# Attention into a snake feed-forward block on one core: opening loads and copies dealt out anew, batch 1's loads and steps reordered

## The chip, the core and the metric

The kernel runs on one core of a Trainium2 chip. The metric is the device time of one execution in microseconds (us), lower is better. Three runs of the kernel before gave 283.33, 283.48 and 284.21 us; their median, 283.48 us, is the time before.

The engines go by the names of the profile: PE is TensorE's matrix multiply and PEld its weight load, DVE is VectorE, ACT is ScalarE, POOL is GpSimd, SP is SyncE, which here only issues transfers. Each engine works through its own list of instructions in the order in which the program names them, and waits at an instruction until its inputs are there and its output buffer is free.

## The reference

Linear attention over 8 batches of 8 heads, 576 positions and 64 columns, and then a feed-forward block with the activation h + sin²(alpha·h)/alpha on the 4608 tokens that come out:

```python
q_s = exp(q - max(q, axis=-1));  q_s = q_s / (sum(q_s, axis=-1) + 1e-09)
k_s = exp(k - max(k, axis=2));   k_s = k_s / (sum(k_s, axis=2) + 1e-09)
kv  = einsum('bhsd,bhse->bhde', k_s, v)
x   = einsum('bhsd,bhde->bhse', q_s, kv)        # (8, 8, 576, 64), taken as 4608 x 512
h   = x @ w_in                                  # w_in 512 x 2048
s   = sin(alpha * h)
g   = h + s * s / (alpha + 1e-09)
out = g @ w_out                                 # w_out 2048 x 512
```

All inputs and the output are float32 in memory; the kernel multiplies in bfloat16.

## The kernel before

**Tiling.** A batch's 576 positions are laid out as 64 groups of 9 (`j`), two heads side by side on the 128 partitions. The feed-forward block runs over 9 token tiles `t` of 512 tokens. For each tile there are 16 blocks `ni` of 128 columns of w_in: `mm_h` (line 254) makes one block of h with four matmuls over the four row blocks `k` of w_in, in the order `KO` = 0, 2, 1, 3. `sine` (line 265) takes the sine on ACT and squares it on ACT, POOL or DVE, and `combine` (line 276) makes g on DVE, which also frees the accumulator bank of h. Then 64 matmuls `mm_o` (line 280), called output products here, multiply g with w_out into four accumulators, and `evac_o` copies and stores them.

**Attention of one batch.** `exp_half` takes exponentials of q or k on ACT, for one half `ii` of the heads. `norm_q` normalises q on DVE and POOL into `qn`. `cast_v0` and `cast_v1` turn v into bfloat16 (`vb`). `kv_mm` (36 small matmuls for a half) multiplies k and v, `kv_norm` divides on DVE and gives `kbd`. `q_transpose_ii` turns `qn` on TensorE, a copy makes `qT` of it. `attn_x` multiplies `qT` and `kbd`, and copies put the result into `xT`, the input of `mm_h`.

**The opening** (lines 305 to 410). SP loads q, k and v of batch 0 in halves. POOL waits for the first half of k (`held`, line 338, a copy of one column whose only use is that the loads behind it on POOL are not issued before) and then issues the second half of v in two parts, and w_in through `load_win`, which converts to bfloat16 on the way: columns 0 to 255 of row blocks 0 and 2, the same columns of row blocks 1 and 3, then 256 columns at a time up to 1023. After its cast of v it issues w_in's columns 1024 to 1535 and 1536 to 2047 and w_out's row blocks 0 to 3 and 4 to 7. TensorE multiplies the blocks `ni` 0 to 3 with row blocks 0 and 2 first ("early products", lines 401 to 410), since `xT` for these is made first, from half 0 of the heads. The main loop adds row blocks 1 and 3 (line 413).

**Tile 0's blocks** (lines 457 to 463). The loop over `ni` issues the blocks; the table `late` (line 457) names loads that are issued behind a block: behind `ni` 6 the first half of batch 1's q on SP, behind 8 and 10 w_out's row blocks 8 to 11 and 12, 13 on POOL, behind 13 the second half of q and all of k and v of batch 1. `load_q1` (line 441) first writes one column on DVE, so that SP's issue waits for DVE's place in the program.

**Batch 1** (lines 465 to 514). `o_quad` hands out tile 0's 64 output products, and `take(os, n)` puts the next n of them on TensorE. The order of the products is written out: products 1 to 16 use w_out's row blocks 0 to 3, 17 to 32 use 4 to 7, 33 to 48 use 8 to 11, 49 to 56 use 12 and 13, the rest 14 and 15. After the first 46 come batch 1's transposes, `kv_mm`, `attn_x` (in `x_half`), with the other 18 between them. Then `mm_h(1, 0)`, the first block of tile 1, follows. Within this stretch POOL makes the first half of `qn`, waits for k's first half (`held`, line 471) and issues w_out's row blocks 14 and 15.

Of the kernel before, what the change touches and what calls it, by code (L numbers as in the profile page):

```python
# [23 lines left out]
def kernel(  # L24
# [23 lines left out]
    MF = 512  # L48
# [57 lines left out]
    def load_win(c0, c1, cc=slice(0, 4)):  # L106
        nc.gpsimd.dma_start(out=win[:, cc, c0:c1], in_=win_v[:, cc, c0:c1])

    def load_wout(n0, n1):
        nc.gpsimd.dma_start(out=wout[:, n0:n1, :], in_=wout_v[:, n0:n1, :])  # L110
# [13 lines left out]
    def exp_half(name, b, ii, j1=J, j0=0):  # L124
        if (name + "e", b) not in A:
            A[name + "e", b] = att2.tile([128, J, 4 * D], BF16, name=name + "e")
        exp_to(A[name + "e", b][:, j0:j1], staged[name, b][:, :, j0:j1], (ii,))
# [10 lines left out]
    def norm_q(b, engs, j1=J):  # L138

        qe = A["qe", b][:, 0:j1].rearrange("p j (ii x d) -> p ii j x d", ii=2, x=2)  # L140
        A["qn", b] = qn = att1.tile([128, 2, J, 2 * D], BF16, name="qn")
        qs = small.tile([128, J, 4], F32, name="qs")
        if len(engs) == 1:
            nc.vector.tensor_reduce(qs, A["qe", b].rearrange("p j (i d) -> p j i d", i=4), axis=AXL.X, op=ALU.add)  # L144
            nc.vector.reciprocal(qs, qs)  # L145
        for ii in range(2):
            part = qs[:, 0:j1, 2 * ii:2 * ii + 2]
            if len(engs) == 2:
                nc.vector.tensor_reduce(part, qe[:, ii], axis=AXL.X, op=ALU.add)  # L149
                nc.vector.reciprocal(part, part)  # L150
            engs[ii % len(engs)].tensor_tensor(qn[:, ii, 0:j1].rearrange("p j (x d) -> p j x d", x=2), qe[:, ii],  # L151
                                               part.unsqueeze(3).to_broadcast([128, j1, 2, D]), op=ALU.mult)
# [101 lines left out]
    def mm_h(t, ni, k0=0, k1=4):  # L254

        if ni == 0 and k0 == 0:
            G[t] = gpool.tile([128, nN, MF], BF16, name="g")
        hp = HP[t, ni] if k0 else bank(BANKS.get(t, 3 * "aabb" + "abba")[ni])
        HP[t, ni] = hp
        for k in range(k0, k1):  # L260
            nc.tensor.matmul(hp, win[:, KO[k], ni * 128:(ni + 1) * 128],  # L261
                             xT[:, KO[k], t * MF % NX:t * MF % NX + MF], start=(k == 0), stop=(k == 3))
        return hp
# [69 lines left out]
    def cast_v0(ii, j0, j1, eng):  # L333
        vv = vb[0].rearrange("p j (i c) -> p i j c", i=4)
        eng(vv[:, 2 * ii:2 * ii + 2, j0:j1, 0:D], staged["v", 0][:, ii::2, j0:j1])  # L335
# [2 lines left out]
    GP_CP(held, staged["k", 0][:, 0, 0, 0:1])  # L338
    load0(GP, "v", v, 1, 0, 5)
    load0(GP, "v", v, 1, 5, 9)  # L340
    for ii in range(2):
        load_win(0, 256, slice(ii, 4, 2))
    for c in range(1, 4):
        load_win(256 * c, 256 * c + 256)

    def warm_up(n):
# [36 lines left out]
    kv_norm(0, 0, 1)  # L383
    tp1 = ps_l.tile([128, 8, 128], BF16, name="tp", tag="l")
    q_transpose_ii(0, 1, 0, 8, tp1)
    cast_v0(1, 0, 5, DVE_CP)
    cast_v0(1, 5, 9, GP_CP)
    for c in range(2, 4):
        load_win(512 * c, 512 * c + 512)
# [2 lines left out]

    xp = [bank("b") for _ in range(2)]
    attn_x(0, 0, 0, 8, xp)
    DVE_CP(xT[:, 0, 0:MF], xp[0])
    ACT_CP(xT[:, 2, 0:MF], xp[1])
    ACT_CP(A["qT", 0][:, 1, 0:8], tp1)
    nc.scalar.activation(zero, zero, AX.Sin)
    kv_mm(0, 1, ps_k, split=True)
    kv_norm(0, 1, 2)  # L400
    for ki in range(2):
        for ni in range(2):
            mm_h(0, ni, ki, ki + 1)
    xp = [bank("l") for _ in range(2)]
    attn_x(0, 1, 0, 8, xp)
    for x in range(2):
        DVE_CP(xT[:, 2 * x + 1, 0:MF], xp[x])
    for ki in range(2):
        for ni in range(2, 4):
            mm_h(0, ni, ki, ki + 1)  # L410

    def h_slot(t, ni, sq, lag):
        hp = mm_h(t, ni, 2 if ni < (4, 1, 0)[min(t, 2)] else 0)
# [18 lines left out]
    def take(it, n=1000):  # L432
        for _ in range(n):
            if next(it, 0) == 0:
                return
# [4 lines left out]
    with ES:  # L440
        def load_q1(ii):
            if ii == 0:
                staged["q", 1] = stage.tile([128, 4, J, D], F32, name="st_q", tag="st")
            st = staged["q", 1]
            DVE_CP(st[:, ii, 0, 0:1], zero)
            nc.sync.dma_start(out=st[:, ii::2, 0:8].rearrange("p i j d -> p i (j d)"),
                              in_=src_view(q, 1)[:, ii::2, 0:8 * D])

        def load_kv1():
            for n in "kv":  # L450
                staged[n, 1] = stage.tile([128, 4, J, D], F32, name=f"st_{n}", tag="st")
            for ii in range(2):
                for n, t in (("k", k), ("v", v)):
                    nc.sync.dma_start(out=staged[n, 1][:, ii::2].rearrange("p i j d -> p i (j d)"),
                                      in_=src_view(t, 1)[:, ii::2])

        late = {6: lambda: load_q1(0), 8: lambda: load_wout(8, 12), 10: lambda: load_wout(12, 14), 13: lambda: (load_q1(1), load_kv1())}
        for ni in range(nN):
            h_slot(0, ni, "DPPAPPAPPAAPPAPD"[ni], lag)
            flush(lag, 1)  # L460
            if ni in late:
                late[ni]()
        flush(lag, 0)

        accs = [bank(kind) for kind in "bbll"]
        os = o_quad(0, accs, [DVE_CP, ACT_CP, DVE_CP, DVE_CP])
        take(os, 46)
        for ii in range(2):
            exp_half("q", 1, ii, 8)
        norm_q(1, [GP, V], 8)  # L470
        GP_CP(held, staged["k", 1][:, 0, 0, 0:1])
        load_wout(14, 16)

        def cast_v1(ii, eng):
            vv = vb[1].rearrange("p j (i c) -> p i j c", i=4)
            eng(vv[:, 2 * ii:2 * ii + 2, :, 0:D], staged["v", 1][:, ii::2])

        exp_half("k", 1, 0)
        cast_v1(0, ACT_CP)
        exp_half("k", 1, 1)  # L480
        def transpose_q1(ii):
            tp = ps_h[0].tile([128, 8, 128], BF16, name="tp", tag="a")
            q_transpose_ii(1, ii, 0, 8, tp)
            DVE_CP(q_tile(1)[:, ii, 0:8], tp)

        transpose_q1(0)
        take(os, 4)

        def x_half(ii):
            xp = [bank("a") for _ in range(2)]  # L490
            attn_x(1, ii, 0, 8, xp)
            for x in range(2):
                (ACT_CP, DVE_CP)[x](xT[:, 2 * x + ii, MF:2 * MF], xp[x])

        kv_mm(1, 0, ps_k, split=True)
        kv_norm(1, 0, 1)
        for b in range(2):
            DVE_CP(q8[:, 0, b, 0:1], zero)
            nc.sync.dma_start(out=q8[:, :, b], in_=src_view(q, b)[:, :, 8 * D:J * D])
        load_batch(2)  # L500
        cast_v1(1, DVE_CP)
        take(os, 4)
        x_half(0)
        take(os, 2)
        transpose_q1(1)
        kv_mm(1, 1, ps_k, split=True)
        kv_norm(1, 1, 2)
        take(os, 5)
        x_half(1)
        exp_to(A["qe", 1][:, J - 2:J], q8)  # L510
        nc.scalar.activation(zero, zero, AX.Sin)
        take(os)
        for ki in range(2):
            mm_h(1, 0, ki, ki + 1)
        norm_q8()
        load("q", q, 3)
        load("k", k, 3)
        load("v", v, 3)

        def late_q8(ni):  # L520
            if ni == 11:
                tp = ps_k.tile([128, 2, 2, 128], BF16, name="tp", tag="a")
                for b in range(2):
                    for ii in range(2):
                        nc.tensor.transpose(tp[:, ii, b], A["qe", 1][:, J - 2 + b, ii * 128:(ii + 1) * 128], identb)
                DVE_CP(A["qT", 1][:, :, J - 2:J], tp)
            elif ni == 15:
                xp = ps_k.tile([128, 2, 512], F32, name="xp", tag="a")
                for ii in range(2):
                    for b in range(2):  # L530
                        for e in range(2):
                            for x in range(2):
                                r, c = slice(64 * x, 64 * x + 64), (2 * ii + b) * P
                                nc.tensor.matmul(xp[64 * e:64 * e + 64, x, c:c + P], kbd[b][r, e, ii],
                                                 A["qT", 1][r, ii, J - 2 + b, e * 64:(e + 1) * 64],
                                                 start=True, stop=True)
                DVE_CP(xT[:, :, 16 * P:18 * P].rearrange("p (x i) n -> p x i n", x=2),
                       xp[:, :, 0:4 * P].rearrange("p x (i n) -> p x i n", i=2))

        for ni in range(nN):  # L540
            h_slot(1, ni, SQ[ni], lag)
            flush(lag, 1)
            late_q8(ni)
        cast_v(2, [GP_CP, GP_CP])
        flush(lag, 0)
# [149 lines left out]
```

## Time and profile before

| what | value |
|---|---|
| runs | 283.33, 283.48, 284.21 us |
| profiled execution | 284.08 us |
| its span on the core | 282.3 us |
| HBM read, written | 36.71 MB, 9.44 MB |
| w_in's pieces, issue to landing | 128 KB: 5.3 us; 256 KB: 7.0 us; 512 KB: 9.8 us (medians) |
| start of tile 0's first output product | 29.34 us |
| start of the first transpose of batch 1 | 39.26 us |
| start of tile 1's first block | 46.46 us |

The span is the time from the first to the last instruction on the core; the profiled execution took 1.8 us more than it. Times in the text are from the span's start. The page gives, for each engine, busy time, share of the span and number of instructions, and rows of 40 digits, the busy tenths of each of 40 slices (7.06 us each). The chain of waits goes back from the last instruction to what released each; its columns are start, duration, and what. In the timeline the columns are start, duration, engine, line, operation, output and inputs, and how many are merged in the row; in brackets stands the idle time before it and what ended it. In the table of windows each engine has its busy time and number of instructions in order PE, PEld, DVE, ACT, POOL; then come the clock granted to TensorE, the DMA engines' busy share (above 1 when transfers overlap in an engine) and GB/s. A landing time is the start of a transfer's issue plus its time to landing, taken from the list of transfers in a window that holds this one issue.

### The profile page before, as it was taken

Reading aid. Unit: us, or ns where it says so; the run is one execution under the profiler, and the core shown is the slowest. Engines: PE = TensorE matmul, PEld = TensorE weight load, DVE = VectorE, ACT = ScalarE, POOL = GpSimd, SP = SyncE. Lnnn points to the kernel's source line nnn. Section 1 sums busy time; section 2 is a strip of 40 time slices with the busy share of each in tenths; the row PEclk is TensorE's granted clock in tenths of the full one; section 3 lists DMA queues with packets and bytes.
Section 4 is the critical chain, followed back from the end, with each engine's and each line's share of the span. In section 5 each row is a group of like instructions: output and inputs, shape, how many; then the busy total and the mean of one; then the engine's idle time right before and its main releaser. Section 6 shows DMA issues by size and latency. Waiting matters only on the chain.

```text
span 282.3 us, 4919 instructions
## 1 busy us (share of the span) xinstructions
PE 267.7 (95%) x1890; PEld 123.7 (44%) x1919; DVE 185.2 (66%) x280; ACT 223.7 (79%) x319; POOL 81.8 (29%) x76
## 2 busy tenths in 40 slices
PE   2789999999999999999999999999999999999994
PEld 1334444444444444444544444444444444444443
DVE  3858758799958767766775677667685555555412
ACT  4879666999588999899989998999877777777400
POOL 1868430777776550025003500341000000000000
PEclk9999999999999999999999999999999999999999
DMA  7999998996799129811992189125011111111143
GB/s 252 290 195 219 286 324 280 383 324 248 159 155 410 62 46 316 339 38 39 236 404 60 37 233 407 35 64 123 0 37 39 37 37 37 39 37 41 43 107 74
DMA packets 39048, 45.82 MB, mean 162 GB/s; under 512 B 16992, under 2 KB 22384, under 8 KB 39024
## 3 DMA queue, kind: packets, MB, share of 16 engines
q1 hardware_dynamic: 33360, 40.57, 46.9%
q0 software_dynamic: 5472, 4.79, 10.4%
q8 instruction: 15, 0.25, 0.4%
q10 hardware_dynamic: 192, 0.14, 0.2%
q14 instruction: 9, 0.07, 0.1%
HBM read 36.71 MB, written 9.44 MB: 163 GB/s over the span
## 4 chain that ended last, share of the span: by engine, by line
PE 85%; DMA 7%; POOL 3%; ACT 2%; issue 1%; DVE 1%; SPq 0%; ACTq 0%
PE op L281 38%; PE hp L261 37%; DMA st_v<-in_v_dram 3%; DMA win<-in_moe_w_in_dram 2%; PE kvp L172 2%; DMA st_k<-in_k_dram 2%; PE lp L261 2%; POOL s L271 1%; PE op L261 1%; PE op L665 1%; ACT s L267 1%; PE hp L216 1%; PE kvp L261 1%; PE xp L216 1%; POOL st_v L306 1%
## 5 line engine op out<-in xcount | busy, mean ns | idle before, releaser
L277 DVE SCALAR_TENSOR_TENSOR g<-s,inva_sb,hp 128x512 bf16<-128x512 f32 x128 | 94.5, 745 | 58.8 <-ACT s L269 53.3
L261 PE MATMUL hp<-xT,win 128*128 128x512 bf16 x505 | 127.5, 379 | 1.3 <-DMA win<-in_moe_w_in_dram 0.9
L281 PE MATMUL op<-wout,g 128*128 128x512 bf16 x478 | 121.0, 379 | 1.6 <-issue 1.1
L267 ACT ACTIVATE s<-hp,alpha_sb 128x512 f32<-128x512 f32 x128 | 86.2, 682 | 24.2 <-PE hp L261 22.9
L261 PEld LDWEIGHTS <-win 128*128 128x128 bf16 x576 | 55.8, 98 | 68.6 <-DMA win<-in_moe_w_in_dram 1.8
L281 PEld LDWEIGHTS <-g 128*128 128x128 bf16 x560 | 53.2, 98 | 64.7 <-issue 2.3
L269 ACT ACTIVATE s<-s 128x512 f32<-128x512 f32 x112 | 70.5, 630 | 3.6
L271 POOL TENSOR_TENSOR s<-s 128x512 f32<-128x512 f32 x29 | 30.1, 1055 | 22.6 <-ACT s L267 22.6
L151 POOL TENSOR_TENSOR qn<-qe,qs 128x1152 bf16<-128x1152 bf16 (+1 forms) x12 | 25.1, 2111 | 33.9 <-DVE qs L145 25.2
L293 DVE COPY o<-op 128x512 f32<-128x512 f32 (+2 forms) x33 | 21.8, 660 | 10.2 <-PE op L281 7.9
L136 POOL CAST vb<-st_v 128x1152 bf16<-128x1152 f32 x12 | 14.7, 1258 | 44.8 <-DMA st_v<-in_v_dram 44.8
L117 ACT ACTIVATE qe<-st_q 128x1152 bf16<-128x1152 f32 (+2 forms) x18 | 17.7, 1025 | 7.0 <-DMA st_q<-in_q_dram 6.9
L117 ACT ACTIVATE ke<-st_k 128x1152 bf16<-128x1152 f32 x16 | 17.9, 1151 | 0.9 <-DMA st_k<-in_k_dram 0.9
L144 DVE TENSOR_REDUCE qs<-qe 128x36 f32<-128x2304 bf16 x5 | 12.8, 2550 | 8.3 <-ACT qe L117 8.3
L117 ACT ACT_TABLE_LOAD x7 | 9.0, 1283 | 1.3 <-PEq L679 1.2
L281 PE MATMUL hp<-wout,g 128*128 128x512 bf16 x31 | 8.8, 379 | 0.1
L281 PE MATMUL lp<-wout,g 128*128 128x512 bf16 x30 | 8.6, 380 | 0.2 <-issue 0.2
L172 PE MATMUL kvp<-vb,ke 64*64 64x65 bf16 x576 | 6.9, 194 | 1.9 <-ACT vb L335 1.2
L172 PEld LDWEIGHTS <-ke 64*64 64x64 bf16 x576 | 5.9, 106 | 5.7 <-issue 3.0
L261 PE MATMUL lp<-xT,win 128*128 128x512 bf16 x31 | 7.5, 379 | 0.1
L229 DVE CAST xT<-xp 128x1024 bf16<-128x1024 f32 (+1 forms) x7 | 7.4, 1065 | 0.0
L149 DVE TENSOR_REDUCE qs<-qe 128x16 f32<-128x1024 bf16 (+1 forms) x4 | 5.1, 1266 | 3.4 <-ACT qe L117 3.4
(87 smaller groups left out, 131.8 us busy)
## 6 DMA issues: line engine op xcount, KB each, us to landing
out_dram<-o SPq DMA_DIRECT2D x70, 128.0 KB, 2.4
st_q<-in_q_dram SPq DMA_DIRECT2D x6, 1152.0 KB, 6.3
st_k<-in_k_dram SPq DMA_DIRECT2D x6, 1152.0 KB, 8.5
st_v<-in_v_dram SPq DMA_DIRECT2D x6, 1152.0 KB, 11.2
st_k<-in_k_dram SPq DMA_DIRECT2D x4, 576.0 KB, 7.7
st_q<-in_q_dram SPq DMA_DIRECT2D x4, 512.0 KB, 6.3
st_v<-in_v_dram SPq DMA_DIRECT2D x3, 576.0 KB, 8.2
wout<-in_moe_w_out_dram POOLq DMA_DIRECT2D x3, 512.0 KB, 12.5
```

Source lines behind the costliest of these rows:

```text
L117: nc.scalar.activation(dst[:, :, ii * 128:(ii + 1) * 128].rearrange("p j (x d) -> p x j d", x=2), src[:, ii::2], AX.Exp)
L136: engs[ii](vv[:, 2 * ii:2 * ii + 2, :, 0:D], staged["v", b][:, ii::2])
L144: nc.vector.tensor_reduce(qs, A["qe", b].rearrange("p j (i d) -> p j i d", i=4), axis=AXL.X, op=ALU.add)
L151: engs[ii % len(engs)].tensor_tensor(qn[:, ii, 0:j1].rearrange("p j (x d) -> p j x d", x=2), qe[:, ii], part.unsqueeze(3).to_broadcast([12 ...
L172: nc.tensor.matmul(kvp[64 * x:64 * x + 64, e, ii * 65:(ii + 1) * 65], ke[r, j, h * 64:(h + 1) * 64], vt[r, j, h * 65:(h + 1) * 65], start= ...
L261: nc.tensor.matmul(hp, win[:, KO[k], ni * 128:(ni + 1) * 128], xT[:, KO[k], t * MF % NX:t * MF % NX + MF], start=(k == 0), stop=(k == 3))
L267: nc.scalar.activation(s, hp, AX.Sin, scale=alpha_sb[:, ni:ni + 1])
L269: nc.scalar.activation(s, s, AX.Square)
L271: nc.gpsimd.tensor_tensor(s, s, s, op=ALU.mult)
L277: nc.vector.scalar_tensor_tensor(G[t][:, ni], in0=s, scalar=inva_sb[:, ni:ni + 1], in1=hp, op0=ALU.mult, op1=ALU.add)
L281: nc.tensor.matmul(acc, G[t][:, ni, j * 128:(j + 1) * 128], wout[:, ni, :], start=(ni == 0), stop=(ni == nN - 1))
L293: eng(o[:, cols], acc)
```

## The change

In the opening, w_in's columns 0 to 511 are loaded as columns 0 to 255 of row blocks 0 and 2, columns 256 to 511 of row blocks 0 and 2, and then columns 0 to 511 of row blocks 1 and 3. The first five columns of v's second half are cast by POOL instead of DVE. `qT`'s second half is copied by DVE, earlier, instead of ACT, and ACT and DVE share each pair of copies into `xT`, so that ACT comes to its load of the sine table with one copy less ahead of it. TensorE runs three early products ahead of `attn_x(0, 1)` and five behind it, instead of four and four.

In tile 0's loop, all of batch 1's loads on SP are issued behind `ni` 11, and w_out's row blocks 12 and 13 are no longer issued behind `ni` 10: POOL issues them later, after a copy of one column of q's second half.

In batch 1's stretch, v's second half is cast by POOL right behind its load of w_out's last rows, instead of by DVE; both halves of q are transposed ahead of the first `kv_mm`; the output products between the steps are handed out as 2, 2, 3, 3, 5 and the rest instead of 4, 4, 2, 5 and the rest.

```diff
-    for ii in range(2):
-        load_win(0, 256, slice(ii, 4, 2))
-    for c in range(1, 4):
+    for c in range(2):
+        load_win(256 * c, 256 * c + 256, slice(0, 4, 2))
+    load_win(0, 512, slice(1, 4, 2))
+    for c in range(2, 4):
         load_win(256 * c, 256 * c + 256)
...
     q_transpose_ii(0, 1, 0, 8, tp1)
-    cast_v0(1, 0, 5, DVE_CP)
+    DVE_CP(A["qT", 0][:, 1, 0:8], tp1)
+    cast_v0(1, 0, 5, GP_CP)
     cast_v0(1, 5, 9, GP_CP)
...
     attn_x(0, 0, 0, 8, xp)
-    DVE_CP(xT[:, 0, 0:MF], xp[0])
-    ACT_CP(xT[:, 2, 0:MF], xp[1])
-    ACT_CP(A["qT", 0][:, 1, 0:8], tp1)
+    for x in range(2):
+        (ACT_CP, DVE_CP)[x](xT[:, 2 * x, 0:MF], xp[x])
     nc.scalar.activation(zero, zero, AX.Sin)
     kv_mm(0, 1, ps_k, split=True)
     kv_norm(0, 1, 2)
-    for ki in range(2):
-        for ni in range(2):
-            mm_h(0, ni, ki, ki + 1)
+    for ni, ki in ((0, 0), (1, 0), (0, 1)):
+        mm_h(0, ni, ki, ki + 1)
     xp = [bank("l") for _ in range(2)]
     attn_x(0, 1, 0, 8, xp)
     for x in range(2):
-        DVE_CP(xT[:, 2 * x + 1, 0:MF], xp[x])
-    for ki in range(2):
-        for ni in range(2, 4):
-            mm_h(0, ni, ki, ki + 1)
+        (ACT_CP, DVE_CP)[x](xT[:, 2 * x + 1, 0:MF], xp[x])
+    for ni, ki in ((1, 1), (2, 0), (2, 1), (3, 0), (3, 1)):
+        mm_h(0, ni, ki, ki + 1)
...
-        late = {6: lambda: load_q1(0), 8: lambda: load_wout(8, 12), 10: lambda: load_wout(12, 14), 13: lambda: (load_q1(1), load_kv1())}
+        late = {8: lambda: load_wout(8, 12), 11: lambda: (load_q1(0), load_q1(1), load_kv1())}
...
             exp_half("q", 1, ii, 8)
+        GP_CP(held, staged["q", 1][:, 1, 0, 0:1])
+        load_wout(12, 14)
         norm_q(1, [GP, V], 8)
...
         exp_half("k", 1, 1)
+        cast_v1(1, GP_CP)
...
-        transpose_q1(0)
-        take(os, 4)
...
+        for ii in range(2):
+            transpose_q1(ii)
+            take(os, 2)
         kv_mm(1, 0, ps_k, split=True)
...
         load_batch(2)
-        cast_v1(1, DVE_CP)
-        take(os, 4)
+        take(os, 3)
         x_half(0)
-        take(os, 2)
-        transpose_q1(1)
+        take(os, 3)
         kv_mm(1, 1, ps_k, split=True)
```

## The prediction

> **What bounds the kernel now.** I read the page first: shares of busy time, then the 40 slices.
>
> ```profile
> PE 267.7 (95%) x1890; PEld 123.7 (44%) x1919; DVE 185.2 (66%) x280; ACT 223.7 (79%) x319; POOL 81.8 (29%) x76
> ...
> PE   2789999999999999999999999999999999999994
> ```
>
> TensorE is busy from the fourth slice to the end. So the change, which ends at about 46 us, is worth what it does to the moment at which TensorE gets through batch 1's steps. My checkpoint is the first matmul of token tile 1 (`mm_h(1, 0)`): 46.46 us in the timeline. What moves it moves the end one to one. Next the chain of waits, up to there:
>
> ```profile
> 9.66 6.40 DMA win<-in_moe_w_in_dram
> ...
> 16.11 2.76 PE hp L261 x12
> ...
> 31.44 8.18 DMA st_v<-in_v_dram
> 39.64 1.18 ACT vb L476
> ```
>
> The chain runs through two transfers: w_in's third piece and v of batch 1. Then the timeline, around TensorE's waits and the transfers from GpSimd:
>
> ```profile
> 16.11 2.76 PE L261 MATMUL hp<-xT,win 128*128 128x512 bf16 x12 [0.91 <-DMA win<-in_moe_w_in_dram]
> ...
> 22.41 6.59 PEld L261 LDWEIGHTS <-win 128*128 128x128 bf16 x32 [0.58 <-DMA win<-in_moe_w_in_dram]
> ...
> 29.34 1.89 PE L281 MATMUL hp<-wout,g 128*128 128x512 bf16 x8
> ...
> 38.50 0.77 POOL L110 DMA_DIRECT2D wout<-in_moe_w_out_dram  x1
> ...
> 39.26 0.61 PE L199 MATMUL tp<-identb,qn 128*128 128x128 bf16 x8
> ...
> 43.87 0.48 PE L172 MATMUL kvp<-vb,ke 64*64 64x65 bf16 x36
> ```
>
> A matmul of 512 columns costs (39.26 - 29.34) / 46 = 0.216. The second row is the one to keep: at 22.41 TensorE waits a second time for w_in, for columns 1024 to 1535 (`ni` 8 to 11). Last, the windows; the last two columns are the DMA engines' share and GB/s:
>
> ```profile
> 12.00:14.00 2.00, 1.43 (x47) 0.83 (x45) 1.19 (x4) 1.95 (x3) 1.10 (x2) 1.00 1.29 147
> 14.00:16.00 2.00, 1.06 (x7) 0.31 (x6) 1.16 (x4) 1.72 (x3) 2.00 (x4) 1.00 1.36 177
> ...
> 20.00:22.00 2.00, 2.00 (x11) 0.88 (x9) 1.70 (x3) 1.94 (x5) 1.65 (x3) 1.00 1.24 206
> ```
>
> The DMA share stays at or above 1.0 from 4 to 40 us. So the transfers are one line of work: a landing comes when the work ahead of it is done, and reordering moves one landing at another's cost.
>
> **The opening.** After `attn_x` at 14.80 TensorE idles 0.91, to 16.11. Now the second piece (rows 0 and 2, columns 256 to 511; 128 KB, issued at 8.95 like the old second piece, which took 5.2 to land) is there at 14.2. All eight early products can run ahead of the third piece: three from 13.83, `attn_x` at 14.80 as before (it waits for kbd at 14.44, unchanged), 0.34 for it, five products, end at 16.22. `ni` 0 is then finished from 16.22 instead of 16.99 (16.11 + 4 x 0.22): **0.77 gained**, if the third piece is there; it came at 16.07.
>
> But `ni` 8 then comes up 0.77 earlier too, at 21.4, and its columns (issued 13.47, 8.9 to land) came at 22.4. That landing moves only by what the third piece saves. Before, all of w_in's first 1024 columns go as 512 byte packets (0.50 MB in 1010 packets, 13 to 16 us); now the third piece goes like the later ones, 1 KB each (0.62 MB in 628, 20 to 23 us). 256 KB take 1.78 at 147 GB/s, 1.48 at 177, 1.27 at 206: a saving of 0.2 to 0.5. I take 0.3, and with the latency before the old wait 0.35 for TensorE. The tile's output product starts at 29.0 instead of 29.34; the rest of the 0.77 becomes a longer wait at `ni` 8.
>
> Here a rule speaks against the change. The Trainium skill, "DMA: Bandwidth & Descriptors", Specifications, puts line rate at 512 B and more per transfer piece. By it the third piece saves nothing and 0.35 would be about 0.05; the rows (147 to 177 against 206 GB/s) say otherwise.
>
> **Edits that I cost at nothing.** v's cast of five columns moves from VectorE (0.49, from 11.96) to GpSimd: 0.62 x 640 / 512 = 0.78, from 11.94 (end of its five issues) to 12.72, inside the 0.97 that GpSimd idled before its other cast at 12.90. Without that cover up to 0.5 for `kv_mm(0, 1)` and the issues behind. qT's copy takes VectorE instead of ACT: 12.33 to 13.0, then xT to 13.7; needed at 14.27 by the third product. ACT's table load (1.28) moves from 14.25 to 13.3 and ends before xT's copies at 15.25, which now run on two engines, done at 15.94 instead of 16.54; needed at 16.22. Without these covers 0.3 each, all of it inside the wait at `ni` 8.
>
> **Batch 1's loads.** SP's six loads now go together after `ni` 11: the marks on VectorE follow the combine of `ni` 10 (ends 28.03 before), so issues start at 27.5 to 28.0, not at 24.27 and 30.52. Nothing queues behind them on SP until q8's loads. What sets q's second half is the line of work: it landed at 30.52 + 6.2 = 36.7, with w_out's rows 12 and 13 (26.67 + 9.7 = 36.4) just ahead. These 256 KB (1.27) now come later, and 0.3 is saved above: q's second half lands at **35.1**. That suits its issue: 28.4 + 6.7, against 6.2 and 6.8 measured.
>
> **The new wait.** w_out's rows 12 and 13 are issued only after GpSimd's `held` copy has seen that half of q. In the old row the copy follows k's landing (38.2) and the issue is at 38.50: so 35.1 + 0.3 = 35.4. Behind it on GpSimd stand qn's first half (1.91, done by 38.2, needed at 38.95), w_out's rows 14 and 15, and v's second cast. On TensorE they are needed for the 49th of the 64 output products: 29.0 + 46 x 0.216, two transposes with their switch (0.45 each), two products = **40.25**. Before, they had landed nearly four us ahead of use.
>
> When do they land? No row shows this very meeting. Lower end: the shortest landing of a GpSimd load, 5.2 to 5.3: 40.7. Upper end: they are served behind all of k and v. The work up to both is the old one less 0.3, and v's second half ended it at 32.47 + 10.0 = 42.5: so 42.2. Two rows lie between. Rows 12 and 13 once met q's second half and the two shared, landing at 36.4 and 36.7; sharing from about 38.5 here gives 41.5. Rows 14 and 15 (38.50 + 5.3 = 43.8) met v's second half and came a full 1.3 behind it, their own 1.27 of work. This row is nearest: same queue, same size, same `held` gate, same k and v in the engines. I take **42.1**.
>
> The skill's same page ("Queues, rings and completion order") says that each DMA engine takes turns between queues packet by packet. By that rule it would be 41.5 and the total 0.6 lower; the row of 38.50 doesn't show such turns.
>
> After it TensorE has 16 products (3.45), two `kv_mm` (0.41 each, 43.87 to 44.28), two `attn_x` (0.34 each), four switches at 0.1: 5.35. Checkpoint 42.1 + 5.35 = 47.45 against 46.46: **1.0 later**. It no longer depends on when the output products began, so the opening's gain is in front of this wait and lost in it. v's second cast (GpSimd, 1.16 by the row of 63.11, two in 2.27) ends at 43.4, and kv_mm needs it at 44.85: hidden. Rows 14 and 15: work ahead up to 43.5, needed at 45.3: hidden. The early transpose of q's second half and the takes 2, 2, 3, 3 add no instruction.
>
> **Sum.** The profiled execution took 284.08, 282.3 of it the span; the median of the runs is 283.48, 0.6 less. I apply the difference to the median: 283.48 + 1.0 = **284.5** (285.1 for an execution like the profiled one).
>
> **Rivals.**
> 1. Rows 12 and 13 land early, at 40.7: then v's second cast decides. 42.2 + 1.16 = 43.35, where `kv_mm(1, 1)` started at 43.87: 0.5 gained, **283.0**; faster up to a landing of 41.1 (46.46 - 5.35), slower from there. For: on other engines of the 16 the queue may be empty earlier. Against: the share of 1.05 in the window from 36 to 38.
> 2. The two queues share, 41.5: 46.85 at the checkpoint, 0.4 later, **283.9**.
> 3. The change does all that it seems to say: q and the weights come early, 0.35 to 0.77 from the opening and the idle of about 1.1 in TensorE's row between 40.1 and 46.5 closed: **282.2**. Against: the transfers' work is the same as before, and v's end at 42.2 alone forbids more than 0.5.
> 4. The opening's 512 byte packets were not the brake: 0 instead of 0.3 there; everything lands 0.3 later, 284.8. It goes with the forecast.
>
> **How the numbers follow.** 0.3% is 0.85 us, about what a measurement of this kernel tells from no change. Forecast (with the fourth case) 0.58, of which 0.45 lies above 284.33 and 0.13 below; sharing 0.12, within; early landing 0.18, of which 0.13 is within and 0.05 faster; the third 0.12, faster. So slower 0.45, within 0.38, faster 0.17. Range: 284.5 with landings 41.6 to 42.8 gives 284.0 to 285.2; down to the early landing and a part of the third, 282.6.
>
> **What would show it.** In the new trace: `ni` 8's weight load waits longer for win than 0.58; the output products start near 29.0; q's second half lands near 35.1; TensorE waits 1 to 2 us for w_out in the 49th output product, which no wait of the old trace does; the checkpoint at about 47.4. I am wrong if w_out's rows 12 and 13 land before 41, or if q's second half comes a good us before 35.

## The result and the profile after

The changed kernel is slower: median 286.88 us (285.99 to 287.84, six runs) against 283.40 us (282.48 to 284.21, six runs); ratio 1.0125, 95% interval 1.0096 to 1.0153, or 3.5 us. Ratios and intervals, here and below, are estimated from the fast runs of both kernels, so a ratio is not the quotient of the two medians beside it. The forecast was 284.5 with a range up to 285.2: the direction and the place were right, the size was too small by a factor of more than three. The profiled execution of the changed kernel took 287.28 us, 285.5 of it the span, 3.2 more than the span before.

First the changed kernel's page, busy shares, TensorE's row and the row of the granted clock:

```profile
PE 269.5 (94%) x1890; PEld 124.2 (43%) x1919; DVE 184.8 (65%) x278; ACT 223.4 (78%) x319; POOL 84.8 (30%) x79
...
PE   2899959999999999999999999999999999999995
...
PEclk9999997999999999999999999999999999999999
```

TensorE's row has a 5 in its sixth slice (36 to 43 us), where a 9 stood, and the clock's row a 7 in the seventh. Both are in batch 1's stretch. The first says that TensorE stood still, the second that it ran slowly afterwards. The chain of waits of the changed kernel (start, duration, what) says for whom:

```profile
27.48 7.38 DMA st_q<-in_q_dram
...
35.44 7.37 DMA wout<-in_moe_w_out_dram
42.81 0.04 issue
42.85 0.59 PE hp L281 x2
```

Before, the chain ran here through v's transfer and ACT's cast. Now it runs through q's second half (issued 27.48, landed 34.86) and, hung onto it by the `held` copy, w_out's row blocks 12 and 13 (issued 35.44, landed 42.81). TensorE's timeline in the changed kernel, with the two points that the prediction set its marks at:

```profile
21.55 2.76 PE L261 MATMUL hp<-xT,win 128*128 128x512 bf16 x12 [0.27 <-DMA win<-in_moe_w_in_dram]
...
28.47 1.89 PE L281 MATMUL hp<-wout,g 128*128 128x512 bf16 x8
...
42.85 0.59 PE L281 MATMUL hp<-wout,g 128*128 128x512 bf16 x2 [2.92 <-DMA wout<-in_moe_w_out_dram]
...
46.16 1.06 PE L281 MATMUL lp<-wout,g 128*128 128x512 bf16 x2
...
49.74 1.03 PE L261 MATMUL kvp<-xT,win 128*128 128x512 bf16 x4
```

The output products begin at 28.47 (before 29.34), the 49th waits 2.92 us, and tile 1's first block begins at 49.74 (before 46.46): 3.28 later, which is the whole difference of the spans (3.2). The row of 46.16 shows a second thing: two products in 1.06 us, where two took 0.59. The windows of the changed kernel, with the granted clock third from the end of each row:

```profile
40.00:42.00 2.00, 0.00 (x0) 0.00 (x0) 0.65 (x1) 1.16 (x1) 0.00 (x0) 1.00 1.00 175
42.00:43.00 1.00, 0.15 (x1) 0.10 (x1) 0.00 (x0) 0.00 (x0) 0.88 (x1) 1.00 0.59 92
43.00:44.00 1.00, 0.86 (x38) 0.50 (x38) 0.09 (x1) 0.00 (x0) 0.28 (x1) 0.86 0.06 10
44.00:45.00 1.00, 0.81 (x2) 0.15 (x1) 0.50 (x4) 0.00 (x0) 0.00 (x0) 0.50 0.00 0
45.00:46.00 1.00, 1.00 (x6) 0.27 (x6) 0.10 (x1) 0.13 (x1) 0.00 (x0) 0.50 0.30 69
46.00:47.00 1.00, 1.00 (x3) 0.15 (x1) 0.59 (x1) 0.45 (x1) 0.00 (x0) 0.50 1.06 202
47.00:48.00 1.00, 1.00 (x39) 0.58 (x39) 0.28 (x2) 0.00 (x0) 0.00 (x0) 0.94 0.71 157
```

About 1 us after work resumed, TensorE's clock was halved for some 3.4 us: by the clock column 0.28 us of the window from 43 to 44, all three from 44 to 47, and 0.12 of the one from 47 to 48. The busy shares count these microseconds like any others; only the clock tells them apart.

### The profile page after: what moved, and what is told of

The parts are those of the page before. It is cut to its first block, busy times and chain, and to the rows that moved or that the text cites. A ratio compares the mean times of both kernels' runs of the same rounds, so it can differ in the third digit from the quotient of the medians.

```text
span 285.5 us, 4923 instructions
## 1 busy us (share of the span) xinstructions
PE 269.5 (94%) x1890; PEld 124.2 (43%) x1919; DVE 184.8 (65%) x278; ACT 223.4 (78%) x319; POOL 84.8 (30%) x79
## 4 chain that ended last, share of the span: by engine, by line
PE 84%; DMA 9%; POOL 2%; issue 1%; DVE 1%; ACT 1%; SPq 0%; POOLq 0%
PE op L281 37%; PE hp L261 36%; DMA st_q<-in_q_dram 3%; DMA wout<-in_moe_w_out_dram 3%; DMA win<-in_moe_w_in_dram 2%; PE kvp L172 2%; DMA st_k<-in_k_dram 2%; PE lp L261 1%; PE op L261 1%; PE op L666 1%; PE hp L216 1%; PE kvp L261 1%; PE hp L281 1%; ACT s L267 1%; PE lp L281 1%
## 5 line engine op out<-in xcount | busy, mean ns | idle before, releaser
L281 PE MATMUL hp<-wout,g 128*128 128x512 bf16 x32 | 9.5, 394 | 3.0 <-DMA wout<-in_moe_w_out_dram 2.9
```

Of the source, the lines that this page charges most:

```text
L281: nc.tensor.matmul(acc, G[t][:, ni, j * 128:(j + 1) * 128], wout[:, ni, :], start=(ni == 0), stop=(ni == nN - 1))
```

## The experiments

The theory after the result: the wait for w_out's row blocks 12 and 13 is the loss, and the clock that falls behind it is a second one. Rivals: batch 1's loads, grouped behind block 11, come late; or the new order of the steps is slow by itself. "Clock low" below counts timed executions whose mean granted clock was under 0.9965; it is 0.992 to 0.994 in those, 0.997 to 1.000 in the others. The kernel before had 10 such of 90; these took 2.3 to 3.2 us longer in the mean than its other executions on the same chip, and none of them was profiled.

### One part undone, one part alone

**e1_rows_early.** The changed kernel with the rows issued behind block 10 again:

```diff
-        late = {8: lambda: load_wout(8, 12), 11: lambda: (load_q1(0), load_q1(1), load_kv1())}
+        late = {8: lambda: load_wout(8, 12), 10: lambda: load_wout(12, 14), 11: lambda: (load_q1(0), load_q1(1), load_kv1())}
...
-        GP_CP(held, staged["q", 1][:, 1, 0, 0:1])
-        load_wout(12, 14)
```

> The changed kernel, but w_out's row blocks 12 and 13 are issued behind block 10 again, without the copy that holds them back. If the late landing of these rows is the loss (wait 2.9 us in the changed kernel, then half clock for 3.2 us, 1.6 lost): no wait for w_out in the output products, granted clock 1.00 from 38 to 50 us, and a total of 282.6 to 283.2, not slower than before. If grouping batch 1's loads behind block 11 is the loss, q comes 1.3 us later still than in the changed kernel and the total stays at 286 or goes above.

284.22 us against 283.58, ratio 1.0026 (0.9996 to 1.0056): not told apart from before. No wait for w_out is left, and tile 1's first block starts at 45.83 in the profiled execution. The median lies 1 us above what I expected: the loads are still grouped, and the first transpose waits 0.30 for q's first half (the run r4 below).

**e3_gate_only.** The kernel before with the rows held back, nothing else:

```diff
-        late = {6: lambda: load_q1(0), 8: lambda: load_wout(8, 12), 10: lambda: load_wout(12, 14), 13: lambda: (load_q1(1), load_kv1())}
+        late = {6: lambda: load_q1(0), 8: lambda: load_wout(8, 12), 13: lambda: (load_q1(1), load_kv1())}
...
+        GP_CP(held, staged["q", 1][:, 1, 0, 0:1])
+        load_wout(12, 14)
         norm_q(1, [GP, V], 8)
```

> The kernel before with one thing changed: w_out's row blocks 12 and 13 are issued behind a copy of q's second half, as in the changed kernel. If this one move is the loss: q's second half lands at about 35.5, rows 12 and 13 at about 43, TensorE waits 2.5 to 3 us for them in the 49th output product, the clock halves behind it, and the total is 286.5 to 287.5. If the loss needs the regrouped loads or the new order of steps as well, the total stays below 285.

286.78 us against 283.58, ratio 1.0096 (1.0061 to 1.0131): the first expectation. This one move is enough for a loss of the changed kernel's size (1.0081 and 1.0125 in its two measurements). The timeline of TensorE in this kernel:

```profile
41.78 0.59 PE L281 MATMUL hp<-wout,g 128*128 128x512 bf16 x2 [2.48 <-DMA wout<-in_moe_w_out_dram]
...
47.91 0.81 PE L261 MATMUL kvp<-xT,win 128*128 128x512 bf16 x3
```

The wait is there without any other part of the change; the rows landed at 41.7, not at the expected 43. In this one execution the clock held, although TensorE stood for 2.48 us; in 7 of the 12 it was low. Those averaged 287.3 us, the other five 285.8.

**r4_regroup_only and s3_q_first_early.** The kernel before with batch 1's loads grouped behind block 11, without and with q's first half left behind block 6; the rows stay behind block 10:

```diff
-        late = {6: lambda: load_q1(0), 8: lambda: load_wout(8, 12), 10: lambda: load_wout(12, 14), 13: lambda: (load_q1(1), load_kv1())}
+        late = {8: lambda: load_wout(8, 12), 10: lambda: load_wout(12, 14), 11: lambda: (load_q1(0), load_q1(1), load_kv1())}
```

That is r4; s3 differs from the kernel before only in the last entry:

```diff
+        late = {6: lambda: load_q1(0), 8: lambda: load_wout(8, 12), 10: lambda: load_wout(12, 14), 11: lambda: (load_q1(1), load_kv1())}
```

> The kernel before with one thing changed: batch 1's six loads on SP go together behind block 11; w_out's row blocks 12 and 13 stay behind block 10. If the regrouping costs nothing by itself: total within 0.3% of before. If q's late first half is a loss: its reduction and the first transpose come late, TensorE waits at the transpose at about 39, and the total is over 284.5.

> The kernel before with batch 1's second half of q and its k and v issued behind block 11 instead of 13; q's first half stays behind block 6. If the regrouping lost its 1.7 us to the late first half of q (wait of 1.4 us at the first transpose): no wait there, and the total is within 0.3% of before. If it lost them to the earlier k and v in the transfers, the total stays above 284.5.

r4: 285.32 us against 283.39, ratio 1.0043 (1.0010 to 1.0077): the second expectation. Its profile shows the wait that this one named, in TensorE's timeline at the first transpose:

```profile
39.54 0.45 PEld L199 LDWEIGHTS <-qn 128*128 128x128 bf16 x8 [1.93 <-POOL qn L151]
39.54 0.62 PE L199 MATMUL tp<-identb,qn 128*128 128x128 bf16 x8 [1.44 <-POOL qn L151]
```

q's first half, issued at 27.05 instead of about 24, is exponentiated from 34.81, reduced from 35.90 and multiplied on GpSimd from 37.58 to 39.49; the transpose needs it. s3 has no such wait, its first transpose follows at 37.86 without a gap: 282.71 against 282.98, ratio 1.0026 (0.9996 to 1.0056), not told apart from before. So, as far as these two runs tell, grouping costs something only through q's first half; their intervals overlap, and each has one profile. In the changed kernel this stays hidden: with rows 12 and 13 out of the way q's first half lands at 33.4.

**s1_steps_no_loads.** The changed kernel with all of batch 1's loads as before, so that the opening and the order of the steps remain:

```diff
-        late = {8: lambda: load_wout(8, 12), 11: lambda: (load_q1(0), load_q1(1), load_kv1())}
+        late = {6: lambda: load_q1(0), 8: lambda: load_wout(8, 12), 10: lambda: load_wout(12, 14), 13: lambda: (load_q1(1), load_kv1())}
...
-        GP_CP(held, staged["q", 1][:, 1, 0, 0:1])
-        load_wout(12, 14)
```

> The changed kernel with all of batch 1's loads (SP's six and w_out's row blocks 12 and 13) at the places of the kernel before; the opening and the new order of batch 1's steps stay. If the loss is in the loads alone: within 0.3% of before, at most 1 us of waiting in TensorE's row between 38 and 46 us (second transpose, for qn). If the new order of the steps loses as well: over 284.5.

283.01 us against 282.98, ratio 1.0009 (0.9991 to 1.0028). Opening and steps together move nothing that shows; the loss is in the loads.

**e4_opening_only.** The opening of the changed kernel, everything from tile 0's loop on as before (all of the diff above `h_slot`).

> The kernel before with the opening of the changed one and nothing of batch 1's part. If the transfers bound the gain (my theory, 0.35): output products start at about 29.0, v's first half for batch 1 lands only 0.3 to 0.5 earlier, total 282.9 to 283.1. If the opening's gain carries whole (0.87 in the changed kernel's start of the output products): total 282.3 to 282.6.

283.38 us against 283.58, ratio 1.0003 (0.9971 to 1.0035). Neither gain can be seen: 0.87 us would be 0.9969, just outside the interval, 0.35 lies inside it and isn't excluded. TensorE's timelines show where it goes. The old opening, in e3_gate_only:

```profile
15.38 2.76 PE L261 MATMUL hp<-xT,win 128*128 128x512 bf16 x12 [0.64 <-DMA win<-in_moe_w_in_dram]
...
28.34 1.89 PE L281 MATMUL hp<-wout,g 128*128 128x512 bf16 x8
```

The new one, in e4_opening_only:

```profile
14.77 2.90 PE L261 MATMUL hp<-xT,win 128*128 128x512 bf16 x12 [0.16 <-PE lp L216]
...
21.47 2.76 PE L261 MATMUL hp<-xT,win 128*128 128x512 bf16 x12 [0.20 <-DMA win<-in_moe_w_in_dram]
...
28.39 1.89 PE L281 MATMUL hp<-wout,g 128*128 128x512 bf16 x8
```

The new opening takes up the products 0.6 earlier, waits again at `ni` 8 for w_in's columns 1024 to 1535, and reaches the output products at the same time, 28.39 against 28.34. Over the four profiles with the old opening this point lies between 27.9 and 29.3, over the nine with the new one between 27.3 and 28.7: a single pair of profiles can't tell a few tenths here.

### The wait and the clock

**e2_fill, r2_fill_again and s2_fill_6.** The changed kernel with idle products, whose results nobody uses, on TensorE in the wait: 12 of them in the first two, 6 in the third. r1_after_again is the changed kernel once more, for a comparison on one chip.

```diff
         for ii in range(2):
             transpose_q1(ii)
+            if ii == 1:
+                idle = ps_k.tile([128, 2, 512], F32, name="kvp", tag="a")
+                for _ in range(12):
+                    nc.tensor.matmul(idle[:, 0], identb, xT[:, 0, 0:MF], start=True, stop=True)
             take(os, 2)
```

> The changed kernel with 12 idle products of 512 columns (2.6 us, results unused) put on TensorE where it waited 2.9 us. The wait's end stays, set by the landing at 42.8. If the slow stretch behind the wait (matmuls at 0.42 instead of 0.216 us) is the clock falling because TensorE stood still, the clock stays at 1.00, the first block of tile 1 starts at about 48.2 instead of 49.7 and the total falls by 1.5 to about 285.4. If the steps behind the wait are slow for another reason (order of the steps, copies, banks), the total stays at 286.9.

> The changed kernel once more, so that it stands beside the next runs on one chip. Total 286.5 to 287 again; a granted clock of about 0.994 in most executions, since TensorE stands still for almost 3 us.

> The changed kernel with the 12 idle products in TensorE's wait, beside the changed kernel on one chip. If the fallen clock is a loss of its own (0.006 of 285 us), this is 1.0 to 1.7 below it and no execution shows a clock under 0.998. If the clock only goes with the wait and costs nothing of its own, the two are the same.

> The changed kernel with 6 idle products (1.3 us) in TensorE's wait instead of 12, so that they never last longer than the wait. If standing still for over 2 us is what lets the clock fall, no execution shows a clock under 0.998 with 1 to 1.6 us left to wait, and the total is 284.8 to 285.5, below the 285.8 to 286.2 of 12. If filling helps nothing, it is 286 again.

e2: 286.19 us, ratio 1.0090 (1.0055 to 1.0126). Its profile does what was expected; TensorE's timeline:

```profile
39.99 2.75 PE L500 MATMUL kvp<-xT,identb 128*128 128x512 bf16 x12
42.86 0.59 PE L281 MATMUL hp<-wout,g 128*128 128x512 bf16 x2
...
48.24 1.03 PE L261 MATMUL kvp<-xT,win 128*128 128x512 bf16 x4
```

The 49th product starts at 42.86, as without filling, and tile 1's first block comes 5.38 behind it instead of 6.89, with the clock at 1.00 throughout. The steps behind the wait are not slow by themselves. But the totals show no such gain: r1 took 286.10, ratio 1.0081 (1.0045 to 1.0116), clock low in 8 of 12; r2 took 285.76, ratio 1.0092 (1.0071 to 1.0113), clock low in none of 12. The median is 0.3 lower, the ratio isn't. That falls between the two expectations and doesn't settle the price of the clock in the total: the wait differs from execution to execution (r1's profile shows 2.04 us), and 12 idle products can last longer than it. In r2's profile the rows landed at 41.3, and the idle products kept TensorE until 41.94. Within r1 the four executions with the full clock averaged 284.5 us, the eight with the low one 286.7; part of that is that a short wait goes with a full clock.

With 6 idle products this objection is gone: 284.58 us against 282.98, ratio 1.0073 (1.0052 to 1.0093), clock low in none of 6, against 13 of 18 in the changed kernel. The median is below the expected 284.8 to 285.5, but the ratio's interval overlaps that of r1 (1.0045 to 1.0116), so a gain in total is likely and not shown. TensorE's timeline:

```profile
41.15 0.59 PE L281 MATMUL hp<-wout,g 128*128 128x512 bf16 x2 [0.60 <-DMA wout<-in_moe_w_out_dram]
...
46.53 1.03 PE L261 MATMUL kvp<-xT,win 128*128 128x512 bf16 x4
```

Again 5.38 from the one to the other. In this profile the wait is all that is left of the loss.

**r3_gate_first_half.** The changed kernel with the rows held back by q's first half:

```diff
-        GP_CP(held, staged["q", 1][:, 1, 0, 0:1])
+        GP_CP(held, staged["q", 1][:, 0, 0, 0:1])
```

> The changed kernel, but the copy that holds back w_out's row blocks 12 and 13 looks at q's first half instead of the second, which lands 1.4 us earlier. If the wait follows the issue: issue at about 34.0, landing 40.7 to 41.4, TensorE waits 0.9 to 1.5, the clock stays at 1.00 in most executions, the first block of tile 1 starts at 46.1 to 46.8 and the total is 283.6 to 284.4. If the landing is set by the work of k and v and not by the issue, it stays at 42.8 and the total at 286 to 287.

285.60 us against 283.39, ratio 1.0073 (1.0043 to 1.0103), clock low in 3 of 12. That lies between the two expectations, nearer to the second, and isn't told apart from r1 (1.0081). The timeline of GpSimd and TensorE:

```profile
33.05 0.77 POOL L110 DMA_DIRECT2D wout<-in_moe_w_out_dram  x1 [0.27 <-issue]
...
41.71 0.59 PE L281 MATMUL hp<-wout,g 128*128 128x512 bf16 x2 [2.40 <-DMA wout<-in_moe_w_out_dram]
...
47.08 1.03 PE L261 MATMUL kvp<-xT,win 128*128 128x512 bf16 x4
```

Issued 2.4 us earlier than in the changed kernel's profile, the rows landed only 1.15 earlier, at 41.66: 8.6 us after the issue instead of 7.4. v's second half, the last of SP's loads, landed at 29.30 + 12.2 = 41.5. k and v were already in the transfer engines, and the request came in with the end of them. In all seven profiles with the rows held back they landed 0.1 to 0.9 us behind v's second half, whenever they had been issued. The last two rows show one thing more: in this execution the clock held at 1.00, and the same steps took 5.37 from the 49th product to tile 1's first block, with no idle products.

## Why the prediction was right and wrong

- **The opening.** The mechanism held: the third piece of w_in no longer stops TensorE, the wait moves to columns 1024 to 1535, and those set the start of the output products. In all nine profiles with the new opening the weight load at `ni` 8 waits for w_in, by 0.4 to 0.9 us, against 0.6 at most in the four with the old one. The 0.3 that 1 KB packets were to save is not seen: the third piece took 5.2 to 6.3 us to land in the nine profiles with the new opening (6.2 in the changed kernel) and 5.0 to 6.4 in the four with the old one (6.4 before), and e4 is 1.0003 times before. The rule that I set aside, the Trainium skill's "DMA: Bandwidth & Descriptors", Specifications, with its line rate from 512 B on, fits these landings better than my reading of the windows, though no run excludes a saving of 0.3. The earlier start in the changed kernel's profile, 0.87, is of the size by which this point differs between profiles of one opening.
- **Edits at nothing.** Right as far as the total tells: s1 (1.0009, 0.9991 to 1.0028) has all of the opening's and of the steps' among them.
- **q's second half.** Forecast 35.1, measured 34.86; the issue of the rows 35.4 against 35.44. The transfers as one line of work carried this far. The sum given beside it, 28.4 + 6.7, doesn't describe what happened: the issue came at 27.48 and the trip took 7.4.
- **The landing of the rows.** Forecast 42.1, measured 42.81 in the changed kernel, 42.05 in r1: a little late. They came behind v's second half, as forecast, by 0.8 and 0.9, less than their own 1.27 of work. v landed at 29.73 + 12.3 = 42.0 and k's second half, issued at 29.18, at 40.2, so the queues may have shared in part, which isn't shown; the rows gained nothing by it.
- **The wait.** 42.1 - 40.25 = 1.85 was forecast, 2.92 measured: 0.7 from the landing, the rest because TensorE reached the 49th product at 39.93, 0.3 ahead of the forecast (the output products began 0.5 ahead of it).
- **The step that failed** is the 5.35 from the landing to the checkpoint: 16 products, two `kv_mm`, two `attn_x` and four switches, all priced from rows at the full clock. The changed kernel needed 6.89 (49.74 - 42.85) and r1's profile 6.92, because the clock fell to half behind the wait; with the clock up the filled kernels needed 5.38 and r3 5.37, which shows that the sum was right for the clock it assumed. Of the 2.3 us by which the checkpoint was missed, 1.5 are this and 0.7 the landing. The old trace couldn't show it: behind the start TensorE's longest standstill there is 1.2 us. The Trainium skill names the danger: "TensorE: Matmul & The Clock Gate", "Why this matters for your kernels", warns of throughput drops from gaps over about 3 us in mid-kernel and gives half the clock as the idle state. I weighed two rules on transfers and not this one; by its figure, though, the forecast wait of 1.85 would have been safe.
- **The range.** Its upper end, 285.2, took 42.8 as the latest landing, which came true, with the same 5.35 behind it.
- **The rivals.** Early landing and full gain: refuted by the wait. Sharing, with a landing at 41.5: the rows of the changed kernel landed at 42.81 and 42.05. That the opening's packets were not the brake: right, as far as the runs tell.

What stays open is how much of the 3.5 us the clock is in the mean; profiles say 1.5 in an execution where it falls, and it fell in 13 of 18, which makes an estimate of 1.1. It stays open too why the kernel before had a low clock in 10 of 90. No version beat the kernel before beyond its interval.

## What to carry to other kernels

A load that waits for another load to land pays its whole trip, 6.5 to 8.6 us here for 256 KB in busy engines; before holding one back, find the first instruction that reads it and compare. When a change makes TensorE stand still, price what comes behind at the half clock too, once the gap nears 2 us, and read the clock column before blaming the steps. And a wait removed early only counts if the next transfer that is needed comes earlier as well; the opening suggests this, by the new wait at `ni` 8.

## What the runs showed of the hardware

The clock doesn't fall at one length of gap. In profiles it fell after TensorE had stood for 2.92 us (changed kernel) and 2.04 (r1), and held after 2.48 (e3) and 2.40 (r3). TensorE's timeline in r1:

```profile
42.09 0.59 PE L281 MATMUL hp<-wout,g 128*128 128x512 bf16 x2 [2.04 <-DMA wout<-in_moe_w_out_dram]
...
49.01 1.03 PE L261 MATMUL kvp<-xT,win 128*128 128x512 bf16 x4
```

It fell about 1 us after work had resumed and stayed at half for some 3.4 us: from 43.7 to 47.1 in the changed kernel, from 43.1 to 46.5 in r1, both worked out from the clock in windows of 1 us. The Trainium skill's "TensorE: Matmul & The Clock Gate", "Part 1: The HAM clock gate", tells of a free-running window of about 3.4 us. The length of the slow stretch agrees with that, while a gap of 2.04 us, under the 3 us of the page's advice, was enough here. Filling the gap with idle products kept the clock up in all 27 timed executions of the filled kernels; without them it was low in 13 of 18 of the changed kernel.
